# Two more wq tiles through the B stage, six w_mod tiles kept on chip, and zero fills dealt anew

## Chip, cores and metric

The kernel runs on one core of one Trainium2 chip. The metric is device time in microseconds (us), median of several executions. Time before: 603.9 us.

## The reference

One decode token goes through a conditioned transformer layer, forward and backward; all gradients are outputs.

```python
mod = (silu(c) @ w_mod).reshape(6, 1024)            # sa, ca, ga, sb, cb, gb
h = layernorm(x) * (1 + ca) + sa
q = h @ wq                                          # 1024 x 4096, 32 heads
x1 = x + ga * (softmax(q k^T) v @ wo)               # window of 4096 keys, 4 kv heads
h = layernorm(x1) * (1 + cb) + sb
out = x1 + gb * ((sigmoid(h @ w_gate) * (h @ w_up)) @ w_down)
# outputs: out, and the gradients of x, k_cache, v_cache, wq, wo, w_gate, w_up, w_down, c, w_mod
```

The gradients of the two caches have 65536 rows for each head, of which 4096 are not zero. The kernel writes those zeros itself, in 120 transfers of 1 MB, here called **fills**. They depend on nothing, so they are dealt over the program as cover: wherever other transfers are few, fills keep the DMA queue busy.

## The kernel before

Everything lives in one on-chip arena of 192 KB a partition; regions are reused as soon as they are free. Stages in order: q and the scores, the N stage (k^T p v for each head), the B stage, folds and the first modulation products, seven feed-forward rounds, the end (gradients of wo, w_mod, wq, and the two caches' windows). Fills are dealt by constants:

```python
NBP = 6                                    # wq tiles that go through B
Z_N = spread(29, 128)                      # fills beside the 128 steps of N
Z_B = spread(29, 43) + [1, 1, 1, 1, 0]     # beside the 48 chunks of B
Z_FOLD = (3, 2, 2)
Z_FFN = [(1, 1, 1, 1)] * 5 + [(1, 1, 2, 2), (2, 2, 1, 1)]   # four places in each round
Z_END = (2, 1, 1, 0, 0)                    # the first stands before the first wo gradient
```

A chunk of B is eight 512-column matmuls, and a fill can hang on one of them:

```python
def bch(n=1):
    ...
    for a in range(4):
        for k in range(2):
            mm = nc.tensor.matmul(bbank[p][k], lhsT=a4[:, p, 4*u+a, :], rhs=wo_t[u][:, a, k*512:(k+1)*512], ...)
    zero(Z_B[nbq - 1 - len(bq)], recent(mm, 3))
```

Section 5 of w_mod (eight tiles of 256 KB, for gb) is loaded once before N and once again at the end:

```python
wm_sec(5, 0, 8, 160)                       # before N; gb in one product
...
def sec(j):                                # at the end, eight times
    w5 = sec_t[j][:, 3*D:4*D]              # filled by sec_load(j)
    ttr(w5, w5, dmod_b4[:, 3*D:4*D], dcs[:, j:j+1])
    outer_dve(sec_t[j], cs_col[:, j:j+1], dmod_b4)
    nc.gpsimd.dma_start(out=dwm_view[:, j, 2*D:6*D], in_=sec_t[j])
```

Below is the joint between the last feed-forward round and the end. A **side unit** is a small job that is put between other work to fill idle engines: eight transposes on TensorE and one copy on ScalarE (`side(n)` runs n of them).

```python
    else:
        zero(z[2] + z[3])                  # last round
side(len(jobs))                            # left-over transposes, each PE + an ACT copy
for p in range(NBP):
    nc.scalar.copy(out=B_t[p], in_=BT_ps[p])        # parked B tiles out of PSUM
dx1b, m2 = layernorm_bwd_col(dln2, ...)             # sum over partitions on TensorE
bcast(dattn_bf, KD, dattn_b, "AV")
# 64 "do" matmuls that read all wo tiles
zero(Z_END[0]); sec_load(0); ...; sec_load(1)
for u in range(4): dwo(u)                  # overwrite the wo tiles and store them, 1 MB each
```

Of the kernel before, what the change touches and what calls it, by code (L numbers as in the profile page):

```python
# [10 lines left out]
P = 128  # L11
# [8 lines left out]
D = 1024  # L20
# [4 lines left out]
HQ = 32  # L25
# [15 lines left out]
def spread(total, n):  # L41
    return [(i + 1) * total // n - i * total // n for i in range(n)]


NBP = 6
NT = 8
NGA = 9
Z_GA = 3
Z_CB = 3
Z_Q = [0] * 6 + [1, 3]  # L50
Z_KC = [0] * 8
Z_SM = 4
Z_N = spread(29, 128)
Z_B = spread(29, 43) + [1, 1, 1, 1, 0]
Z_FOLD = (3, 2, 2)
Z_FFN = [(1, 1, 1, 1)] * 5 + [(1, 1, 2, 2), (2, 2, 1, 1)]
Z_END = (2, 1, 1, 0, 0)
@with_exitstack
def kernel(
# [266 lines left out]
    wo_t = [ar(o, 8).rearrange("p (a n) -> p a n", a=4) for o in wo_off]  # L326
    B_off = [156, 158, 152, 154, 156, 158]
    junk = vt([P, D], "junk", BF16)
    B_t = [ar(o, 2) for o in B_off[:5]] + [junk]

# [9 lines left out]

    def mod_tiles(ps, tiles, ts_, first):
        for t in ts_:
            for k in range(KD):
                nc.tensor.matmul(ps[:, k:k + 1], lhsT=tiles[t][:, k * P:(k + 1) * P],
                                 rhs=cs_bf[:, t:t + 1], start=(first and t == ts_[0] and k == 0), stop=(t == KD - 1),
                                 skip_group_check=True)
# [136 lines left out]
    for ch in range(8):  # L483
# [9 lines left out]
        zero(Z_KC[ch], mm)  # L493
    g_t = [ar(160 + 2 * t, 2) for t in range(KD)]
    wm_sec(5, 0, 8, 160)
    load_wo(2)
    mx = vt([P, 1], "mx")
    nc.vector.reduce_max(out=mx, in_=mx8, axis=AX.X)
# [108 lines left out]

    def mod_gb():
        ps = new_ps("g_ps")
        mod_tiles(ps, g_t, range(KD), True)  # L610
        cp(gb, ps[:, 0:KD])
        mulv(dffn_bf, go_col, gb)
        load_wo(0)
        load_wo(1)

# [8 lines left out]
    for g in range(G):  # L624
        nbank = bank_pair("n_ps", g)
        for t_ in range(KT):
# [14 lines left out]
            if s == 2:  # L641
                ok_cols(ok4)
            elif s == 4:
                ok_rows()
            elif s == 24:
                mod_gb()
            elif t_ % 2 == 1:
                side()
# [23 lines left out]
    chunks(4, range(8))  # L672
    chunks(5, range(8))
    nbq = len(bq)
    bbank = {}
# [96 lines left out]
    nc.scalar.activation(out=warm, in_=ones_f[:, 0:1], func=ACT.Sigmoid)  # L772
    bch(len(bq) - 16)
    b_sec(4, 0, 16)
# [29 lines left out]
    b_sec(3, 0, 32)  # L804
    park(2, pna, "na")
    park(3, pna, "na")
    v = A3_ps[:, 0:48].rearrange("p (j n) -> p j n", j=KD)
# [18 lines left out]
    bch(5)  # L826
    assert not bq
    b_sec(3, 4, 40)
    zero(Z_CB)
    rot[:] = [(psum, "mm"), (prq, "rq")]  # L830

    def tr_unit(blk):
        def run():
            tp = new_tp("tp_side")
            for i in range(8):
                nc.tensor.transpose(tp[:, i * P:(i + 1) * P], blk[:, i * P:(i + 1) * P], ident_bf[:, :])  # L836
            nc.scalar.copy(out=blk, in_=tp[:, :])  # L837
        return run

    jobs[:] = [tr_unit(v_nat[:, i // 4, (i % 4) * 1024:(i % 4 + 1) * 1024]) for i in range(16)]  # L840
    side(1)
    park(4, ppq, "pq")
    side(3)

# [29 lines left out]

    def fold_tile(t):
        w2 = w2_t[t]
        for k in range(2):
            ps = new_ps("fold_ps")
            for i in range(4):
                nb = 4 * k + i  # L880
                for x, src in enumerate((ga_t[t], cb_t[t], sb_t[t])):
                    nc.tensor.matmul(ps[:, i * P:(i + 1) * P], lhsT=src[:, nb * P:(nb + 1) * P], rhs=ident_bf[:, :],
                                     start=(i == 0 and x == 0), stop=(x == 2), skip_group_check=True)
            fold_ps.append(ps)
        for k in range(2):
            nc.scalar.copy(out=w2[:, k * 512:(k + 1) * 512], in_=fold_ps[k][:, :])
        fold_ps.clear()

    load_wd(0, 0)
    load_wd(0, 1)  # L890
    fold_ps = []
    md_ps = new_acc("md_ps")
    for t in range(4):
        fold_tile(t)
    mod_tiles(md_ps, sb_t, range(4), True)
    load_ug(0, 0, 4)
    load_ug(0, 4, 4)
    zero(Z_FOLD[0])
    side(2)
    mod_tiles(md_ps, sb_t, range(4, 8), False)  # L900
    cp(sb_, md_ps[:, 0:KD])
    h2 = vt([P, KD], "h2")
    mulv(h2, ln2, cb1)
    addv(h2, h2, sb_)
    h2_bf = vt([P, KD], "h2_bf", BF16)
    cp(h2_bf, h2)
    for t in range(4, 8):
        fold_tile(t)
    park(5, prq, "rq")
    rot[:] = [(psum, "mm")]  # L910
    load_ug(1, 0, 4)
    load_ug(1, 4, 4)
    zero(Z_FOLD[1])
    bcast(dffn_bf, KD, b1k, "AV")

# [57 lines left out]
    for h in range(HQ):  # L973
        jobs.append(tr_unit(wo_t[h // 4][:, h % 4, :]))
    for g in range(G):
        jobs.append(tr_unit(N_sb[:, g * 1024:(g + 1) * 1024]))
# [14 lines left out]
    for q in range(NB):  # L991
        z = Z_FFN[q]
        more = q + 1 < NB
        for j in range(KD):
            w = ug_v[:, q % 2, j // 4, j % 4, :, :].rearrange("p k f -> p (k f)")
            ttr(w, w, dug_b, dh2acc[:, q * KD + j:q * KD + j + 1])
            if j in (0, 2, 5) or (j == 6 and q < 4):
                side()
            outer_act(w, h2[:, j:j + 1], dug_b)
            if j == 0:  # L1000
                if q == 0:
                    cp(ffn, ffn_ps)
                else:
                    addv(ffn, ffn, ffn_ps)
            if j == 3:
                store_ug(q, 0, 4)
                zero(z[0])
            if j == 5:
                store_ug(q, 4, 2)
# [31 lines left out]

    B_t = [ar(o, 2) for o in (40, 42, 44, 152, 154, 156)]
    for p in range(NBP):
        nc.scalar.copy(out=B_t[p], in_=BT_ps[p][:, :])
# [52 lines left out]
    def sec(j):  # L1097
        w5 = sec_t[j][:, 3 * D:4 * D]
        ttr(w5, w5, dmod_b4[:, 3 * D:4 * D], dcs[:, j:j + 1])
        outer_dve(sec_t[j], cs_col[:, j:j + 1], dmod_b4)  # L1100
        nc.gpsimd.dma_start(out=dwm_view[:, j, 2 * D:6 * D], in_=sec_t[j])
# [52 lines left out]

    zero(Z_END[0])
    sec_load(0)
    do_ps = new_ps("do_ps")[:, 0:HQ]
    dov = do_ps.rearrange("p (b a h) -> p b a h", b=2, a=4)
    for b in range(2):
        for hh in range(4):  # L1160
            nc.tensor.matmul(dov[:, b, :, hh], lhsT=do_sb[b][:, hh * P:(hh + 1) * P], rhs=ident_f[:, 0::32],
                             start=True, stop=True)
    sec_load(1)
    for u in range(4):
# [20 lines left out]
    dcs234 = matvec_T(lambda jb, nb: w2_t[jb][:, nb * P:(nb + 1) * P], dh2_hl, "dcs234")  # L1185
    for j in range(2, 5):
        sec_load(j)
    dh1b_ps = new_acc("dh1b_ps")
    for j in range(NBP, NT):
        for h in range(HQ):  # L1190
            nc.tensor.matmul(dh1b_ps[:, j:j + 1], lhsT=a4[:, j, h, :], rhs=do_bf[:, h:h + 1],
                             start=(h == 0), stop=(h == HQ - 1))
    for j in range(5, 8):
        sec_load(j)
    dwo(6)
    sec(0)
    cp(dh1[:, NBP:NT], dh1b_ps[:, NBP:NT])
    DO_hd = make_hd(lambda g: do_pv[:, g, :], "DO_hd")
# [23 lines left out]
    addv(dx0, dx0b, dx1)  # L1222
    sec(3)
    for ch in range(8):
        ps = new_ps("dp_ps")
# [90 lines left out]
```

## Time and profile before

| | before |
|---|---|
| time, median | 603.9 us (603.5 to 605.1) |
| profiled span | 602.8 us |
| moved | 248.19 MB, mean 412 GB/s |
| busiest engine | TensorE, 65% of the span |
| first w_up/w_gate product | at 293.5 us |
| first wo gradient stored | at 486.7 us |

The page gives the busy share of the DMA engines in 40 slices; the table of windows gives busy time by stage; the chain and the timeline give single instructions. The prediction below shows these lines.

### The profile page before, as it was taken

How to read it: one execution, taken by the hardware profiler on the slowest of the kernel's cores; microseconds unless marked ns; L12 is line 12 of the kernel's file. 1: busy time of each engine (PE TensorE's matmuls, PEld its weight loads, DVE VectorE, ACT ScalarE, POOL GpSimd, SP SyncE). 2: the span in 40 equal slices, each digit the busy share in tenths (PEclk: the TensorE clock that was granted, in tenths of full speed). 3: DMA queues.
4: the chain of work that ended last, by engine and by line, in shares of the span. 5: the costliest groups of instructions: out<-in, count | busy, mean ns of one | idle time of the engine just before them, and what ended most of it. 6: DMA issues, size and time to landing. Idle time of an engine off the chain costs nothing.

```text
span 602.8 us, 10936 instructions
## 1 busy us (share of the span) xinstructions
PE 389.8 (65%) x4516; PEld 265.6 (44%) x4516; DVE 324.8 (54%) x616; ACT 282.8 (47%) x426; POOL 174.2 (29%) x281
## 2 busy tenths in 40 slices
PE   3997789999999989989433434352533377837200
PEld 3995434334344445548433433342433255736200
DVE  3654498999511010060374675846768279678510
ACT  2489514567202014218273847657476834744100
POOL 0002121212322212213334454455443431132230
PEclk9999699999999989989755555555555586655555
DMA  8999999999999999999999999999999999999996
GB/s 351 421 417 421 406 426 413 413 417 422 421 422 427 423 426 419 407 426 417 406 413 411 412 415 413 413 409 410 414 416 421 422 419 411 423 424 426 424 415 256
DMA packets 47730, 248.19 MB, mean 412 GB/s; under 512 B 5629, under 2 KB 5629, under 8 KB 27264
## 3 DMA queue, kind: packets, MB, share of 16 engines
q0 software_dynamic: 37792, 210.78, 91.0%
q1 hardware_dynamic: 9840, 36.71, 18.0%
q8 instruction: 35, 0.57, 0.4%
q14 instruction: 15, 0.12, 0.1%
q10 hardware_dynamic: 48, 0.01, 0.0%
HBM read 61.87 MB, written 185.60 MB: 411 GB/s over the span
## 4 chain that ended last, share of the span: by engine, by line
DMA 35%; PE 34%; DVE 14%; issue 7%; ACT 5%; POOL 2%; ACTq 0%; POOLq 0%; DVEq 0%; SPq 0%
DMA out_dram<-arena 17%; PE b_ps L687 14%; DMA out_dram<-zeros 8%; DMA arena<-in_B_w_down_dram 7%; PE n_ps L635 6%; DVE arena L210 4%; DVE arena L193 4%; PE t_ps L597 2%; DMA arena<-in_B_w_up_dram 2%; DVE arena L206 2%; DVE junk L210 2%; ACT arena L241 2%; PE tp_wq L453 2%; PE w_ps L394 1%; PE tp_k L434 1%
## 5 line engine op out<-in xcount | busy, mean ns | idle before, releaser
L169 POOL DMA_DIRECT2D out_dram<-zeros x112 | 61.1, 546 | 205.6 <-PE q_ps L471 50.2
L687 PE MATMUL b_ps<-arena 128*128 128x512 bf16 x384 | 89.5, 389 | 0.0
L836 PE MATMUL tp_side<-ident_bf,arena 128*128 128x128 bf16 x416 | 50.1, 297 | 53.7 <-ACT arena L837 44.6
L193 DVE TENSOR_TENSOR arena<-arena 128x2048 bf16<-128x2048 bf16 x64 | 76.6, 1224 | 2.2 <-PE n_ps L635 0.3
L837 ACT COPY arena<-tp_side 128x1024 bf16<-128x1024 bf16 x52 | 52.0, 1010 | 46.0 <-PE tp_side L836 45.8
L210 DVE CUSTOM_DVE_ANT_0 arena<-arena,scr 128x1024 bf16<-128x1024 bf16 x56 | 65.2, 1221 | 9.5 <-ACT scr L970 9.5
L635 PE MATMUL n_ps<-arena 128*128 128x512 bf16 x256 | 65.7, 378 | 6.5 <-DVE arena L193 4.8
L836 PEld LDWEIGHTS <-arena 128*128 128x128 bf16 x416 | 41.2, 137 | 59.2 <-issue 59.1
L241 ACT ACTIVATE arena<-scr,h 128x1024 bf16<-128x1024 bf16 x56 | 61.0, 1146 | 0.0
L687 PEld LDWEIGHTS <-arena 128*128 128x128 bf16 x384 | 37.7, 100 | 46.4 <-issue 7.1
L873 POOL DMA_DIRECT2D out_dram<-arena x42 | 30.7, 733 | 43.9 <-ACT arena L241 36.7
L635 PEld LDWEIGHTS <-arena 128*128 128x128 bf16 x256 | 24.6, 97 | 41.8 <-issue 16.4
L210 DVE CUSTOM_DVE_ANT_0 junk<-arena,b1k 128x1024 bf16<-128x1024 bf16 x28 | 34.3, 1223 | 15.9 <-DMA arena<-in_B_w_down_dram 15.4
L1137 ACT ACTIVATE arena<-ps_kv 128x512 bf16<-128x512 f32 x48 | 26.2, 694 | 29.8 <-PE ps_kv L1133 26.0
L599 ACT CAST arena<-t_ps 128x512 bf16<-128x512 f32 x56 | 30.1, 589 | 12.1 <-PE t_ps L597 12.1
L1133 PE MATMUL ps_kv<-junk,arena 8*128 8x128 bf16 x256 | 27.5, 306 | 10.1 <-DVE arena L206 9.4
L1133 PEld LDWEIGHTS <-arena 8*128 8x128 bf16 x256 | 25.5, 141 | 11.9 <-issue 11.9
L202 DVE CAST arena<-b_ps 128x512 bf16<-128x512 f32 x5 | 3.5, 692 | 47.1 <-PE b_ps L687 47.1
L933 PE MATMUL fg<-h_bf,arena 128*128 128x1 bf16 x448 | 15.6, 166 | 19.0 <-DMA arena<-in_B_w_up_dram 12.4
L455 ACT COPY arena<-tp_wq 128x1024 bf16<-128x1024 bf16 x23 | 21.7, 1044 | 8.0 <-PE tp_wq L453 8.0
L950 PE MATMUL fg<-hh_bf,arena 128*128 128x1 bf16 x224 | 8.0, 166 | 24.1 <-DMA arena<-in_B_w_down_dram 23.4
L933 PEld LDWEIGHTS <-arena 128*128 128x128 bf16 x448 | 14.4, 105 | 20.2 <-DMA arena<-in_B_w_up_dram 13.0
(297 smaller groups left out, 640.0 us busy)
## 6 DMA issues: line engine op xcount, KB each, us to landing
out_dram<-zeros POOLq DMA_DIRECT2D x112, 1024.0 KB, 13.9
out_dram<-arena POOLq DMA_DIRECT2D x32, 1024.0 KB, 18.8
out_dram<-arena POOLq DMA_DIRECT2D x36, 512.0 KB, 10.3
arena<-in_A_wq_dram SPq DMA_DIRECT2D x8, 1024.0 KB, 20.0
out_dram<-zeros POOLq DMA_DIRECT2D x8, 960.0 KB, 13.1
arena<-in_B_w_down_dram SPq DMA_DIRECT2D x14, 512.0 KB, 9.7
out_dram<-arena POOLq DMA_DIRECT2D x28, 256.0 KB, 10.9
arena<-in_A_wo_dram SPq DMA_DIRECT2D x6, 1024.0 KB, 24.8
```

Source lines behind the costliest of these rows:

```text
L169: ins = nc.gpsimd.dma_start(out=region.bitcast(FP32), in_=zeros[:, :])
L193: return nc.vector.tensor_tensor(out=out, in0=a, in1=b, op=op)
L210: return nc.vector.tensor_tensor_reduce(out=out, in0=w, in1=b, scale=1.0, scalar=0.0, op0=ALU.mult, op1=ALU.add, accum_out=acc)
L241: return nc.scalar.activation(out=out, in_=b, func=ACT.Copy, scale=col)
L599: nc.scalar.copy(out=o, in_=ps)
L635: mm = nc.tensor.matmul(nbank[k][:, :], lhsT=k_nat[:, g, t_ * DH:(t_ + 1) * DH], rhs=vp[:, t_ % 2, 4 * k:4 * k + 4, :].rearrange("p h d -> ...
L687: mm = nc.tensor.matmul(bbank[p][k][:, :], lhsT=a4[:, p, h, :], rhs=wo_t[u][:, a, k * 512:(k + 1) * 512], start=(i == 0 and a == 0), stop= ...
L836: nc.tensor.transpose(tp[:, i * P:(i + 1) * P], blk[:, i * P:(i + 1) * P], ident_bf[:, :])
L837: nc.scalar.copy(out=blk, in_=tp[:, :])
L873: nc.gpsimd.dma_start(out=ug_part(view, q, j0, n), in_=ug_tile(q, k, j0, n))
L933: nc.tensor.matmul(gu[:, col + i:col + i + 1], lhsT=ug_v[:, q % 2, j // 4, j % 4, k, f0:f0 + 255:2], rhs=h2_bf[:, j:j + 1], start=(j == 0) ...
L1133: nc.tensor.matmul(ps[:, t4 * DH:(t4 + 1) * DH], lhsT=rows[32 * g:32 * g + HG, t_ * P:(t_ + 1) * P], rhs=hd[32 * g:32 * g + HG, :], start= ...
```

## The change

It means to save the second load of six section-5 tiles. For that it needs a place to keep them through the feed-forward rounds. It gets one by sending wq tiles 6 and 7 through B as well, which frees their 16 KB a partition before the rounds. The gradient part of those two tiles then comes out of B and not out of a second product at the end. The fills are dealt anew for the longer B stage.

```diff
-NBP = 6
+NBP = 8
-Z_CB = 3
+Z_CB = 1
-Z_N = spread(29, 128)
-Z_B = spread(29, 43) + [1, 1, 1, 1, 0]
-Z_FOLD = (3, 2, 2)
-Z_FFN = [(1, 1, 1, 1)] * 5 + [(1, 1, 2, 2), (2, 2, 1, 1)]
-Z_END = (2, 1, 1, 0, 0)
+Z_N = spread(31, 128)
+Z_B = spread(29, 43) + [1, 1, 1, 1, 0] + [1, 1, 0, 1, 1, 0, 1, 1] + [1, 1, 1, 0, 1, 0, 0, 0]
+Z_FOLD = (0, 4, 3)
+Z_FFN = [(1, 1, 0, 1)] * 5 + [(1, 1, 1, 1), (1, 2, 1, 1)]
+Z_END = (1, 1, 1, 0, 0)
...
-    g_t = [ar(160 + 2 * t, 2) for t in range(KD)]
-    wm_sec(5, 0, 8, 160)
+    g_t = [ar(o, 2) for o in (48, 50, 52, 54, 56, 58, 160, 162)]
+    wm_sec(5, 6, 2, 160)
...
+    chunks(6, range(8))
+    chunks(7, range(8))
...
+    fold_run(range(4), 8)            # folds of w2 with B chunks between them
+    wm_sec(5, 0, 4, 48)              # where wq tile 6 stood
...
+    fold_run(range(4, 8), 6)
+    mod_gb((0, 1, 2, 3))
+    wm_sec(5, 4, 2, 56)              # where wq tile 7 stood
+    load_ug(1, 0, 4); load_ug(1, 4, 4); zero(Z_FOLD[1])
+    side(3)
+    mod_gb((4, 5))
+    mulv(dffn_bf, go_col, gb)
...
-        w5 = sec_t[j][:, 3 * D:4 * D]
+        w5 = g_t[j] if j < 6 else sec_t[j][:, 3 * D:4 * D]
-    sec_load(0)          # and 1 to 5, spread over the first wo gradients
...                      # the second dh1 product (64 matmuls) goes, sec_load(6) and (7) stay
```

More of the change, by code (lines that the diff above doesn't have):

```diff
@@ L326 @@
     wo_t = [ar(o, 8).rearrange("p (a n) -> p a n", a=4) for o in wo_off]
-    B_off = [156, 158, 152, 154, 156, 158]
+    B_off = [156, 158, 152, 154, 156, None, 158, 60]
     junk = vt([P, D], "junk", BF16)
-    B_t = [ar(o, 2) for o in B_off[:5]] + [junk]
+    B_t = [junk if o is None else ar(o, 2) for o in B_off]
     def wo_dram(t, u):
@@ L339, in wm_sec, with mod_tiles @@
                             in_=wm_view[:, j:j + n, sct * D:(sct + 1) * D])
-    def mod_tiles(ps, tiles, ts_, first):
+    def mod_tiles(ps, tiles, ts_, first, last=KD - 1):
         for t in ts_:
@@ L344, in mod_tiles @@
                 nc.tensor.matmul(ps[:, k:k + 1], lhsT=tiles[t][:, k * P:(k + 1) * P],
-                                 rhs=cs_bf[:, t:t + 1], start=(first and t == ts_[0] and k == 0), stop=(t == KD - 1),
+                                 rhs=cs_bf[:, t:t + 1], start=(first and t == ts_[0] and k == 0), stop=(t == last),
                                  skip_group_check=True)
@@ L493 @@
         zero(Z_KC[ch], mm)
-    g_t = [ar(160 + 2 * t, 2) for t in range(KD)]
-    wm_sec(5, 0, 8, 160)
+    g_t = [ar(o, 2) for o in (48, 50, 52, 54, 56, 58, 160, 162)]
+    wm_sec(5, 6, 2, 160)
     load_wo(2)
+    load_wo(1)
     mx = vt([P, 1], "mx")
@@ L606, with mod_gb @@
     dffn_bf = vt([P, KD], "dffn_bf", BF16)
-    def mod_gb():
+    def mod_gb(ts_):
         ps = new_ps("g_ps")
-        mod_tiles(ps, g_t, range(KD), True)
-        cp(gb, ps[:, 0:KD])
-        mulv(dffn_bf, go_col, gb)
-        load_wo(0)
-        load_wo(1)
+        mod_tiles(ps, g_t, ts_, True, ts_[-1])
+        if ts_[0] == 6:
+            cp(gb, ps[:, 0:KD])
+        else:
+            addv(gb, gb, ps[:, 0:KD])
     ok4 = ok_sums()
@@ L645 @@
             elif s == 24:
-                mod_gb()
+                mod_gb((6, 7))
+                load_wo(0)
             elif t_ % 2 == 1:
@@ L772 @@
     nc.scalar.activation(out=warm, in_=ones_f[:, 0:1], func=ACT.Sigmoid)
-    bch(len(bq) - 16)
+    bch(len(bq) - 32)
     b_sec(4, 0, 16)
@@ L804 @@
     b_sec(3, 0, 32)
-    park(2, pna, "na")
-    park(3, pna, "na")
     v = A3_ps[:, 0:48].rearrange("p (j n) -> p j n", j=KD)
@@ L826, with tr_unit @@
     bch(5)
-    assert not bq
     b_sec(3, 4, 40)
     zero(Z_CB)
-    rot[:] = [(psum, "mm"), (prq, "rq")]
-    def tr_unit(blk):
+    def tr_unit(blk, dst=None):
         def run():
@@ L836, in run @@
                 nc.tensor.transpose(tp[:, i * P:(i + 1) * P], blk[:, i * P:(i + 1) * P], ident_bf[:, :])
-            nc.scalar.copy(out=blk, in_=tp[:, :])
+            nc.scalar.copy(out=blk if dst is None else dst, in_=tp[:, :])
         return run
-    jobs[:] = [tr_unit(v_nat[:, i // 4, (i % 4) * 1024:(i % 4 + 1) * 1024]) for i in range(16)]
-    side(1)
-    park(4, ppq, "pq")
-    side(3)
     wg_view = B_w_gate.rearrange("(j p) n -> p j n", p=P)
@@ L873, in store_ug, with fold_half, fold_run @@
             nc.gpsimd.dma_start(out=ug_part(view, q, j0, n), in_=ug_tile(q, k, j0, n))
-    def fold_tile(t):
-        w2 = w2_t[t]
-        for k in range(2):
-            ps = new_ps("fold_ps")
-            for i in range(4):
-                nb = 4 * k + i
-                for x, src in enumerate((ga_t[t], cb_t[t], sb_t[t])):
-                    nc.tensor.matmul(ps[:, i * P:(i + 1) * P], lhsT=src[:, nb * P:(nb + 1) * P], rhs=ident_bf[:, :],
-                                     start=(i == 0 and x == 0), stop=(x == 2), skip_group_check=True)
-            fold_ps.append(ps)
-        for k in range(2):
-            nc.scalar.copy(out=w2[:, k * 512:(k + 1) * 512], in_=fold_ps[k][:, :])
-        fold_ps.clear()
-    load_wd(0, 0)
-    load_wd(0, 1)
-    fold_ps = []
+    def fold_half(t, k):
+        ps = new_ps("fold_ps")
+        for i in range(4):
+            nb = 4 * k + i
+            for x, src in enumerate((ga_t[t], cb_t[t], sb_t[t])):
+                nc.tensor.matmul(ps[:, i * P:(i + 1) * P], lhsT=src[:, nb * P:(nb + 1) * P], rhs=ident_bf[:, :],
+                                 start=(i == 0 and x == 0), stop=(x == 2), skip_group_check=True)
+        nc.scalar.copy(out=w2_t[t][:, k * 512:(k + 1) * 512], in_=ps[:, :])
+    def fold_run(tiles, n):
+        units = [(t, k) for t in tiles for k in range(2)]
+        for i, (t, k) in enumerate(units):
+            if (i + 1) * n // 8 > i * n // 8:
+                bch(1)
+            fold_half(t, k)
+    h2 = vt([P, KD], "h2")
     md_ps = new_acc("md_ps")
-    for t in range(4):
-        fold_tile(t)
+    fold_run(range(4), 8)
     mod_tiles(md_ps, sb_t, range(4), True)
@@ L897 @@
     load_ug(0, 4, 4)
-    zero(Z_FOLD[0])
-    side(2)
+    wm_sec(5, 0, 4, 48)
+    park(2, pna, "na")
+    park(3, pna, "na")
+    load_wd(0, 0)
+    bch(2)
     mod_tiles(md_ps, sb_t, range(4, 8), False)
     cp(sb_, md_ps[:, 0:KD])
-    h2 = vt([P, KD], "h2")
     mulv(h2, ln2, cb1)
@@ L906 @@
     cp(h2_bf, h2)
-    for t in range(4, 8):
-        fold_tile(t)
-    park(5, prq, "rq")
-    rot[:] = [(psum, "mm")]
+    fold_run(range(4, 8), 6)
+    mod_gb((0, 1, 2, 3))
+    assert not bq
+    wm_sec(5, 4, 2, 56)
     load_ug(1, 0, 4)
@@ L913 @@
     zero(Z_FOLD[1])
+    park(4, ppq, "pq")
+    park(5, prq, "rq")
+    tr_unit(B_t[6], ar(62, 2))()
+    load_wd(0, 1)
+    jobs[:] = [tr_unit(v_nat[:, i // 4, (i % 4) * 1024:(i % 4 + 1) * 1024]) for i in range(16)]
+    side(3)
+    mod_gb((4, 5))
+    mulv(dffn_bf, go_col, gb)
     bcast(dffn_bf, KD, b1k, "AV")
@@ L974 @@
         jobs.append(tr_unit(wo_t[h // 4][:, h % 4, :]))
+    jobs.append(tr_unit(B_t[7]))
     for g in range(G):
@@ L996 @@
             ttr(w, w, dug_b, dh2acc[:, q * KD + j:q * KD + j + 1])
-            if j in (0, 2, 5) or (j == 6 and q < 4):
+            if j in (0, 2, 5, 6):
                 side()
@@ L1039 @@
     side(len(jobs))
-    B_t = [ar(o, 2) for o in (40, 42, 44, 152, 154, 156)]
-    for p in range(NBP):
+    B_t = [ar(o, 2) for o in (40, 42, 44, 152, 154, 156, 62, 60)]
+    for p in range(6):
         nc.scalar.copy(out=B_t[p], in_=BT_ps[p][:, :])
@@ L1162 @@
                              start=True, stop=True)
-    sec_load(1)
     for u in range(4):
@@ L1185 @@
     dcs234 = matvec_T(lambda jb, nb: w2_t[jb][:, nb * P:(nb + 1) * P], dh2_hl, "dcs234")
-    for j in range(2, 5):
-        sec_load(j)
-    dh1b_ps = new_acc("dh1b_ps")
-    for j in range(NBP, NT):
-        for h in range(HQ):
-            nc.tensor.matmul(dh1b_ps[:, j:j + 1], lhsT=a4[:, j, h, :], rhs=do_bf[:, h:h + 1],
-                             start=(h == 0), stop=(h == HQ - 1))
-    for j in range(5, 8):
-        sec_load(j)
     dwo(6)
     sec(0)
-    cp(dh1[:, NBP:NT], dh1b_ps[:, NBP:NT])
     DO_hd = make_hd(lambda g: do_pv[:, g, :], "DO_hd")
@@ L1223 @@
     sec(3)
+    sec_load(6)
+    sec_load(7)
     for ch in range(8):
```

## The prediction

> **What bounds the kernel now.** I read the slices of the page first, then the table of windows by stage, then the waits, then the timeline of one feed-forward round and of the tail.
>
> The page, whole span in 40 slices of 15.07 us (the first two lines are busy share of the DMA engines and what they moved), and the totals:
>
> ```profile
> DMA  8999999999999999999999999999999999999996
> GB/s 351 421 417 421 406 426 413 413 417 422 421 422 427 423 426 419 407 426 417 406 413 411 412 415 413 413 409 410 414 416 421 422 419 411 423 424 426 424 415 256
> DMA packets 47730, 248.19 MB, mean 412 GB/s; under 512 B 5629, under 2 KB 5629, under 8 KB 27264
> HBM read 61.87 MB, written 185.60 MB: 411 GB/s over the span
> ```
>
> The transfers run at nine tenths or more in 38 of the 40 slices, and at 406 to 427 GB/s whatever the stage. Only the first slice (start-up) and the last (drain) fall short. No engine comes near: the busiest, TensorE, has 65% of the span. 248.19 MB at the 38 full slices' mean of about 417 GB/s take 595 us of a 603 us span. So the kernel is a transfer of 248 MB, with compute arranged beside it.
>
> The same by stage (columns: window, its length, busy us and instructions of PE, PEld, DVE, ACT, POOL; granted clock; DMA share; GB/s):
>
> ```profile
> 60.00:157.00 97.00, 85.39 (x485) 38.44 (x485) 82.91 (x94) 46.84 (x113) 19.95 (x36) 0.95 1.16 416
> 157.00:271.00 114.00, 108.14 (x791) 55.12 (x790) 23.36 (x57) 23.26 (x34) 26.91 (x46) 0.97 1.14 421
> 271.00:293.00 22.00, 18.27 (x324) 16.58 (x323) 0.57 (x4) 15.44 (x23) 8.37 (x14) 1.00 1.16 412
> 345.00:370.00 25.00, 10.63 (x158) 9.14 (x156) 16.38 (x34) 16.27 (x19) 12.03 (x18) 0.50 1.13 413
> 580.00:603.00 23.00, 0.00 (x0) 0.00 (x0) 0.00 (x0) 0.00 (x0) 2.13 (x4) 0.50 0.76 307
> ```
>
> The reader is to see two balances. From 157 to 271 us (the B stage, and the loads and sums beside it) TensorE works 108 of 114 us: this stretch is as long as its matmuls, and the zero fills of the caches are dealt out beside them so that the queue stays full. In one feed-forward round (345 to 370) no engine has more than 16.4 of 25 us: there the transfers set the pace. After 580 nothing computes: the queue drains.
>
> The waits of the whole span say the same from the other side, as the GpSimd queue that issues most transfers waits for earlier transfers:
>
> ```profile
> POOL out_dram L169 <- DMA out_dram<-zeros: 27.0, 16, 2.1
> POOL arena L869 <- DMA out_dram<-zeros: 11.7, 7, 2.2
> ```
>
> A zero fill (L169) reads nothing that a zero fill writes, so I take these waits for room in the queue: the issuer runs up to 2 us ahead of a full queue.
>
> **What the Trainium skill says.** "DMA: Bandwidth & Descriptors", Specifications, names 435 GB/s as the fabric ceiling and about 358 GB/s as the limit of memory for one core. The trace fits the first (427 in its best slice) and not the second (412 over the span), so the measured rate is used. The same page, Anatomy of one DMA, says that DMA engines do not wait on semaphores, that such waits happen on the issuing sequencer; so a late producer shows as an idle issuer, and hurts only if the queue behind it runs empty. Here the issuer does wait for matmuls (38.5 us for b_ps at L169) and the slices stay full. "TensorE: Matmul & The Clock Gate", Part 2, gives 216 ns between 512-column bf16 matmuls; the chain of this kernel shows eight b_ps matmuls in 1.73 us, which is 216 ns. Its Part 1 has the clock halved after idle windows; the trace grants 0.97 in the B stage and 0.50 in the feed-forward rounds, where TensorE is mostly idle, so where matmuls are added matters: these are added where the clock is high.
>
> **The change part by part.**
>
> (a) *Bytes.* Before, section 5 of w_mod (eight 128x1024 bf16 tiles, 262,144 bytes each) is loaded twice: 2 MB before the N stage for gb, and again eight times 256 KB near the end for its gradient. After, tiles 0 to 5 are loaded once, between B and the feed-forward part, and stay; only 6 and 7 are loaded twice. Removed: 6 x 0.262 = 1.57 MB of reads, nothing added. I counted the zero fills from the constants: 119 plus one left for the end before, 120 after; the same 120 regions. 248.19 becomes 246.62 MB. At 417 GB/s: **1.57 / 0.417 = 3.8 us less**, 0.6% of the time.
>
> (b) *Matmuls.* Two more tiles of wq through the B stage: 2 x 8 x 4 x 2 = 128 matmuls of 512 columns in 16 chunks of 1.73 us: **27.7 us more TensorE work**, all before the feed-forward part. Gone: 64 one-column matmuls of the second dh1 sum; the 64 of the gb product in the timeline took 1.59 us, so some 1.6 us, less 16 that are added elsewhere. Two extra transposed tiles (8 transposes, 0.61 us, and a 1.0 us copy each), one in this stretch and one as side work. The gb product is split into pieces of 16, 32 and 16 matmuls; its sum stays 1.6 us, of which 1.2 move behind B. Three side units instead of six run before the feed-forward part (-1.8 us of TensorE). Net for 157 to 293: about +27.5 us.
>
> (c) *What covers those 27.5 us.* The zero fills are dealt anew: N +2, B +10 (33 to 43), the place after B -2, folds -1 before the first feed-forward product and +1 behind it, feed-forward rounds -8 (32 to 24), the end -1, the leftover -1. Between N and the first feed-forward product the queue gets 7 fills (7.34 MB) and 1.57 MB of gb tiles more: 8.9 MB / 0.417 = 21.4 us. That stretch was 136.4 us long (157 to 293.4, the first matmul at L933) with TensorE busy for 126.4; after, 136.4 + 21.4 = 157.8 us of transfers beside some 154 us of matmuls. Compute still fits, with about 4 us to spare instead of 10: the tightest place of the change.
>
> (d) *The rounds get shorter.* A round moves 3.15 MB in, 3.15 MB out and four fills of 1.05 MB: 10.5 MB / 0.413 = 25.4 us, and in the chain the rounds follow each other by 25.2 us (the wait for w_down ends at 352.66 and 377.86). With three fills: 9.44 / 0.413 = 22.9 us. The end loses 1.57 MB of loads and two fills. So B ends late and everything behind it catches up: the shifts are of 20 us and more, the sum is the bytes.
>
> On the path that sets the end lies only (a). The waits removed at the end (the loads before sec) cost nothing today: they are SyncE's, and DVE's longest idle times there are for output tiles to leave.
>
> **Rivals.**
>
> *1. Compute becomes the bound of the rounds.* In the round around 370 us, DVE sits idle 2.84 us until w_down lands:
>
> ```profile
> 371.39 0.16 DVE L193 TENSOR_TENSOR hh_bf<-sg,fg 128x4 bf16<-128x4 f32 x1 [4.47 <-ACT om L939]
> 377.86 1.23 DVE L210 CUSTOM_DVE_ANT_0 junk<-arena,b1k 128x1024 bf16<-128x1024 bf16 x1 [2.84 <-DMA arena<-in_B_w_down_dram]
> ```
>
> Take that and TensorE's 0.90 us wait for w_gate away from 25.2 and the chain through ScalarE's copies and outer products, the gates and DVE's reductions is some 21.5 us. The new round needs 22.9 by bytes. The margin is 1.4 us; rounds 5 and 6 get one more side unit than today (about 1 us on ScalarE) but still have three or more fills. If the chain were 24 us instead, six rounds would lose 6 us and the gain would turn into +3: about 606.
>
> *2. The stretch after B starves the queue.* The last two gb tiles go where tile 7 of wq stood, so their load waits for the last B chunk, and the matmuls for them wait for the load, before dffn, its broadcast and the first round. A load takes some 10 to 14 us to land. Behind it stand two w_up/w_gate loads of 1 MB and four fills, 6.3 MB or 15 us, and 1 MB of w_down: enough cover by my count, so I expect TensorE to stand still there for 5 to 10 us without the queue running dry. If it did run dry, 2 to 5 us would be lost: 602 to 605.
>
> *3. The gain is larger.* Fewer, better placed loads near the end could shorten the drain (307 GB/s in the last 23 us). But the last outputs are the same; I give it 1 us at most: 599.
>
> *4. The removed loads were hidden anyway.* On a queue that is full throughout nothing is hidden: a byte saved is time saved. I reject it; it would leave 603.9.
>
> **Range and chances.** 603.9 - 3.8 = 600.1; a little back for thinner cover (rivals 1 and 2 at part strength) gives 600.4. The range: 598.2 (all of it and a better drain) to 603.6 (nearly all lost to gaps). A gain over 2% would need 12 us, and the whole shortfall of first and last slice plus the bytes is not more than that: 0.01. A loss of over 2% needs 12 us of empty queue: 0.03.
>
> **What would show each step right or wrong.** The page's total should be 246.6 MB with read 60.3 and written 185.6; slices 2 to 39 at nine tenths, 406 to 427 GB/s. 512 b_ps matmuls instead of 384, mean still near 216 ns apart at a clock near 1. The first L933 product at about 315 to 323 us instead of 293; rounds about 23 us apart; no section 5 loads at the end but two. Wrong would be: slices of 7 or 8 around 300 to 325 (rival 2), rounds of over 23.5 us with DMA share falling and DVE's wait for w_down gone (rival 1), a granted clock of 0.5 in the added chunks (27.7 us would become 55 and the queue would run dry), or a rate below 405 GB/s from the new mixture of loads and fills.

## The result

The changed kernel takes **610.06 us** (608.13 to 611.04, six runs) against 603.92 us (603.49 to 605.06, six runs): 1.0% slower, with a ratio of 1.0096 (95% interval 1.0074 to 1.0117). A ratio here is the mean time of one kernel's runs over that of the other's of the same rounds, so not quite the ratio of the two medians. Executions over 1.5% slower than the fastest of the same kernel are left out of the means. The prediction had 600.4 us, and 603.6 at the most.

The page of the changed kernel, the lines that answer to those of before:

```profile
DMA  9999999999999999999999999999999998999996
GB/s 350 420 418 422 415 424 417 425 419 419 423 424 427 423 427 419 417 424 429 400 412 392 423 409 412 410 412 412 412 411 409 377 369 309 407 421 424 424 417 270
DMA packets 46899, 246.64 MB, mean 407 GB/s; under 512 B 5565, under 2 KB 5565, under 8 KB 26432
HBM read 60.30 MB, written 185.60 MB: 406 GB/s over the span
```

The bytes went as predicted, 246.64 MB and 60.30 MB of reads. But there is a trough of 377, 369 and 309 GB/s in slices 32 to 34, from 470 to 515 us, where the kernel before had 411 to 422. It has two parts. The small one is at 475 to 480 us: 294 GB/s, after the issuer had waited 7.45 us for ScalarE. The large one lies behind it; narrow windows of the changed kernel there (window; length; busy us and instructions of PE, PEld, DVE, ACT, POOL; granted clock; DMA share; GB/s):

```profile
490.00:498.00 8.00, 3.05 (x28) 1.53 (x32) 1.71 (x10) 5.49 (x7) 0.00 (x0) 0.50 1.14 425
498.00:502.00 4.00, 4.00 (x99) 2.38 (x92) 2.82 (x7) 1.17 (x2) 0.80 (x1) 0.94 0.06 14
502.00:510.00 8.00, 5.66 (x101) 5.34 (x98) 7.94 (x24) 4.01 (x8) 3.25 (x4) 0.71 0.93 338
510.00:520.00 10.00, 5.50 (x204) 5.25 (x207) 7.60 (x18) 2.12 (x3) 2.60 (x4) 0.50 1.02 372
```

For four microseconds the queue is all but empty, and for another 18 the transfers stay slow. The same place of the kernel before, 15 us earlier in the program's time:

```profile
480.00:490.00 10.00, 9.48 (x141) 5.83 (x141) 7.05 (x23) 3.10 (x6) 3.19 (x5) 0.75 1.14 425
490.00:500.00 10.00, 5.38 (x158) 4.97 (x156) 8.03 (x25) 3.97 (x8) 4.05 (x6) 0.76 1.08 412
```

What GpSimd issued there, from the timeline (start, length, what; in brackets the idle time before it and what ended it). First before:

```profile
478.25 0.53 POOL L169 DMA_DIRECT2D out_dram<-zeros  x1 [1.87 <-DMA out_dram<-zeros]
480.69 1.83 POOL L169 DMA_DIRECT2D out_dram<-zeros  x3 [1.91 <-DMA out_dram<-zeros]
486.71 0.80 POOL L1106 DMA_DIRECT2D out_dram<-arena  x1 [4.19 <-DVE arena L206]
```

then after:

```profile
482.46 1.45 POOL L868 DMA_DIRECT2D out_dram<-arena  x2 [1.72 <-ACT arena L241]
483.91 2.68 POOL L169 DMA_DIRECT2D out_dram<-zeros  x5
501.15 0.80 POOL L1111 DMA_DIRECT2D out_dram<-arena  x1 [14.56 <-DVE arena L206]
```

Before, the issuer waited for earlier transfers (a full queue) and the first wo gradient came 6 us after the last fills. After, five fills went out at once at 483.9 (the issuer had waited for ScalarE, not for the queue), 12.6 us of transfers by 5 x 1.05 MB / 0.417, and then nothing until 501.15. The landing time of the eight wo gradients (issue to landing, min/median/max) tells how much stood in the queue ahead of them, before and after:

```profile
DMA to landing us min/median/max: 14.2/20.4/23.8
```

```profile
DMA to landing us min/median/max: 6.6/9.7/14.3
```

### The account of the shift

Three times from the timelines carry it. The first w_up/w_gate product moves from 293.5 to 321.0 us (+27.5), the first wo gradient from 486.7 to 501.2 (+14.5). So the compute between them took 193.2 us and now takes 180.1: 13.1 less. Of this the rounds gained 17.4 (293.5 to 446.4 before, 321.0 to 456.6 after: from the first product to the long matmul group of the seventh round), and the joint lost about 4. The transfers dealt into that stretch fell by more: eight fills in the rounds and one in front of the first wo gradient less, one more behind the first product, 8 x 1.05 = 8.39 MB, or 20.1 us. 20.1 - 13.1 = **7.0 us without cover**. The profiled run is 3.5 us longer than before and has 3.8 us of bytes less, so 7.3 us went missing.

That the two agree is partly luck: the subtraction leaves out what stood in the queue at either end. The traces allow a direct count. Up to its first wo store the kernel before had moved 202 MB (486.7 us at 415 GB/s), the changed one 206 MB (501.15 us at 411). The 14.4 us more thus moved 4.0 MB, worth 9.6 us at 417 GB/s: some 4.8 us were lost by then and the other 2.5 behind it. These are estimates from rounded rates, good to about 1 us. And the profiled run was the fastest of the six, 608.13 us; on the mean of the runs 5.8 + 3.8 = 9.6 us went missing.

### The profile page after: what moved, and what is told of

Its sections match the earlier page's. It is cut to its first block, busy times and chain, and to the rows that moved or that the text cites.

```text
span 606.3 us, 11103 instructions
## 1 busy us (share of the span) xinstructions
PE 414.7 (68%) x4587; PEld 278.8 (46%) x4612; DVE 326.2 (54%) x619; ACT 285.4 (47%) x430; POOL 176.4 (29%) x283
## 2 busy tenths in 40 slices
DMA packets 46899, 246.64 MB, mean 407 GB/s; under 512 B 5565, under 2 KB 5565, under 8 KB 26432
## 3 DMA queue, kind: packets, MB, share of 16 engines
HBM read 60.30 MB, written 185.60 MB: 406 GB/s over the span
## 4 chain that ended last, share of the span: by engine, by line
PE 43%; DMA 26%; DVE 13%; ACT 10%; issue 5%; POOL 0%; ACTq 0%; POOLq 0%; SPq 0%; DVEq 0%
PE b_ps L691 17%; DMA out_dram<-arena 13%; PE n_ps L636 6%; DMA arena<-in_B_w_down_dram 4%; DMA out_dram<-zeros 4%; ACT arena L241 4%; DVE arena L193 4%; DVE arena L206 3%; DMA arena<-in_w_mod_dram 3%; PE t_ps L598 2%; PE ps_kv L1138 2%; DVE arena L210 2%; PE tp_wq L453 2%; PE w_ps L394 1%; PE fold_ps L875 1%
## 5 line engine op out<-in xcount | busy, mean ns | idle before, releaser
L691 PE MATMUL b_ps<-arena 128*128 128x512 bf16 x494 | 114.4, 381 | 1.2 <-issue 0.4
L836 PE MATMUL tp_side<-ident_bf,arena 128*128 128x128 bf16 x432 | 53.0, 300 | 59.7 <-ACT arena L837 51.6
L837 ACT COPY arena<-tp_side 128x1024 bf16<-128x1024 bf16 x54 | 54.5, 1009 | 39.3 <-PE tp_side L836 38.9
L877 ACT CAST arena<-fold_ps 128x512 bf16<-128x512 f32 x16 | 9.4, 586 | 29.4 <-PE fold_ps L875 29.4
L206 DVE TENSOR_SCALAR arena<-arena,cs_col 128x4096 bf16<-128x4096 bf16 (+1 forms) x16 | 16.0, 1017 | 8.9 <-DMA out_dram<-arena 8.8
```

What stands on the lines that cost most here:

```text
L206: return nc.vector.tensor_scalar(out=out, in0=a, scalar1=s1, scalar2=None, op0=op0)
L691: mm = nc.tensor.matmul(bbank[p][k][:, :], lhsT=a4[:, p, h, :], rhs=wo_t[u][:, a, k * 512:(k + 1) * 512], start=(i == 0 and a == 0), stop= ...
L836: nc.tensor.transpose(tp[:, i * P:(i + 1) * P], blk[:, i * P:(i + 1) * P], ident_bf[:, :])
L837: nc.scalar.copy(out=blk if dst is None else dst, in_=tp[:, :])
```

## The experiments

The changed kernel itself was not timed again beside them; each run was timed against the kernel before on its own chip. I compare runs by their ratios to the kernel before, a hundredth being 6.0 us; the changed kernel stands at 1.0096 (1.0074 to 1.0117). With four runs each, an interval reaches some 1 to 2 us to either side, so smaller differences are called noise unless the runs themselves keep apart. Theory A says that the first wo gradient comes too late and leaves the queue empty; it began with the added matmuls as the cause of the lateness, and that half fell. Its rival, theory B, says that the loss is spread over the dealing of the fills and the late load of the gb tiles, and that the hole is only where it shows.

### 1. Fills of the end moved into the hole

```diff
-Z_END = (1, 1, 1, 0, 0)
+Z_END = (3, 0, 0, 0, 0)
```

> Changed kernel, with the three zero fills of the end stage (1,1,1 before, between and after the first wo gradients) all put before the first of them. Theory A (the added matmuls lengthen the path of compute up to the first wo gradient, about 501 us; the queue, empty from 498 to 502 us there, is refilled only by what is left): the two fills, 5 us of transfers, fall into the gap and leave the later end, so 3 to 5 us faster than the changed kernel's 610: 605 to 607, first wo gradient still stored at 500 to 502 us. Theory B (the loss is spread: thin queue in the feed-forward rounds and before them; the gap is only where it shows): within 1 us of 610.

Measured: 607.14 us (606.71 to 610.74), ratio 1.0070 (1.0036 to 1.0103), or 1.6 us better than the changed kernel by the ratios, which is not clear of noise. The first wo gradient was stored at 502.4. In the profile the hole from 498 to 502 us is closed (422 GB/s), but new ones stand at 510 to 540 us (375, 392 and 348 GB/s), where the two fills now were missing, and at 330 to 340 us (329 GB/s). So closing this hole won little, while the loss reappeared elsewhere; the run alone does not decide between A and B.

### 2. The six tiles loaded again

```diff
-        w5 = g_t[j] if j < 6 else sec_t[j][:, 3 * D:4 * D]
+        w5 = sec_t[j][:, 3 * D:4 * D]
+    sec_load(0) ... sec_load(5)      # at the places of the kernel before
```

> Changed kernel, but the six tiles of section 5 are loaded again at the end, where the kernel before loads them, and used from there: all of the 1.57 MB come back. If bytes on a full queue still set the time (my prediction's step a): 3.8 us slower than the changed kernel, 614. Theory A (the queue is empty or thin from 498 to 520 us, when these loads are issued): they cost nothing or at most 1.5 us: 609 to 611.5.

Measured: 611.69 us (611.43 to 611.9), ratio 1.0128 (1.0113 to 1.0143), so 1.9 us slower than the changed kernel. That is between the two, and the intervals overlap, so how much of the 3.8 us of bytes is hidden stays open. What it does show: with the removed loads put back the kernel is not faster, so their absence is not what opened the hole. Runs 12 and 13 ask about the bytes again on a full queue.

### 3. A quarter of the added matmuls

```diff
-            for a in range(4):
+            heads = range(4) if p < 6 else (0,)
+            for a in heads:
```

> Wrong result on purpose (two columns blocks of one gradient and what follows from them): changed kernel, tiles 6 and 7 of wq do only a quarter of their matmuls in B, so 96 of the 128 added matmuls, 20.7 us of TensorE, go; all transfers and the places of all fills stay. Theory A: the path of compute up to the first wo gradient gets about 20 us shorter as far as the queue lets it, the queue stays full at the joint, and the time falls to what the bytes allow, 600 +- 1.5 us. Theory B (the dealing of the fills and the late load of the gb tiles leave the holes, the matmuls do not): 607 or more.

Measured: 608.87 us (608.13 to 609.38), ratio 1.0080 (1.0065 to 1.0095), only 1.0 us better than the changed kernel and within the noise. Theory A as first put, with the matmuls as its root, failed here; the "607 or more" of theory B came true. The wait view of TensorE in this stretch and the start of the first product say why:

```profile
PE g_ps L344 <- DMA arena<-in_w_mod_dram: 14.5, 2, 13.3
```

```profile
320.31 1.89 PE L938 MATMUL fg<-h_bf,arena 128*128 128x1 bf16 x64
```

With 20.7 us of matmuls gone, the first product still starts at 320.3: TensorE now waits 13.3 us in one go for a gb tile that stands in the queue behind the fills of B. In the changed kernel no such wait is seen: its matmuls end only about when that tile is there. Two limits tie there. That became theory A2: matmuls and transfers together hold the first product, and behind it the compute up to the first wo gradient takes longer than the transfers that are left as cover.

### 4. A shorter path at the joint

No transfer and no fill changes place in the program. The left-over side units and most copies of the parked tiles (B tiles that waited in PSUM) go behind the layernorm sum, the broadcast and the `do` matmuls, and VectorE alone copies the broadcast out. In the changed kernel the broadcast had stood behind those copies:

```profile
494.95 1.01 PE L297 MATMUL bc_ps<-ident_bf,dattn_bf 128*128 128x128 bf16 x8 [6.27 <-ACT arena L1049]
```

```diff
-    side(len(jobs))
-    for p in range(6): nc.scalar.copy(out=B_t[p], in_=BT_ps[p])
+    rot[:] = [(psum, "mm")]
     dx1b, m2 = layernorm_bwd_col(...)
-    bcast(dattn_bf, KD, dattn_b, "AV")
+    bcast(dattn_bf, KD, dattn_b, "VV")
+    for p in range(2): nc.scalar.copy(out=B_t[p], in_=BT_ps[p])
+    rot[:] = [(pgu, "gu"), (px, "x")]
     # do matmuls
+    for p in range(2, 6): nc.scalar.copy(out=B_t[p], in_=BT_ps[p])
+    side(len(jobs))
```

> Changed kernel with a shorter path from the last feed-forward round to the first wo gradient: the four left-over side units and the copies of the parked tiles are moved behind the layernorm sum, the broadcast of dattn and the do matmuls. No transfer and no fill changes place in the program. Theory A: the first wo gradient is stored 8 to 13 us earlier (488 to 493 instead of 501), the queue no longer runs dry, and the time falls by 5 to 9 us: 601 to 605. Theory B: at most 2 us faster, 608 or more.

Measured: 603.86 us (603.44 to 606.2), ratio 1.0006 (0.9987 to 1.0026), 5.4 us better than the changed kernel, clear of noise. What GpSimd issued, and the window where the changed kernel had 14 GB/s:

```profile
484.44 2.68 POOL L169 DMA_DIRECT2D out_dram<-zeros  x5
489.23 0.80 POOL L1114 DMA_DIRECT2D out_dram<-arena  x1 [2.10 <-DVE arena L206]
```

```profile
498.00:502.00 4.00, 4.00 (x29) 4.00 (x27) 0.37 (x5) 0.06 (x1) 0.00 (x0) 0.50 1.04 408
```

The fills go out at the same time as before the edit, the first wo gradient follows 5 us behind them, and the hole is gone. This is the run that shows where most of the loss arose.

### 5. The control: the same shorter path in the kernel before

> Control: the kernel before with the same shorter path from the last feed-forward round to the first wo gradient as in the run that had it on the changed kernel. There the queue was full at that place, so the path was hidden. Theory A (a path of compute costs only where the queue runs dry): first wo gradient about 10 us earlier in the program's order, time within 1 us of the kernel before, 603 to 605. If the path itself sets the time in both kernels: 5 us or more faster, below 599.

Measured: 603.66 us (603.57 to 604.75), ratio 0.9995 (0.998 to 1.001): no change. What GpSimd issued:

```profile
480.69 3.25 POOL L169 DMA_DIRECT2D out_dram<-zeros  x3 [1.76 <-DMA out_dram<-zeros]
483.93 1.52 POOL L1109 DMA_DIRECT2D out_dram<-arena  x2
```

The edit took: VectorE began the first wo gradient at 476.4 us instead of 484.7. But its store stood in the issuer behind the fills, which waited for room, and went out only 2.8 us earlier (483.9 against 486.7), not the 10 that I expected of the program's order. The same path is free where the queue is full and cost 5.4 us where it was empty.

### 6 and 7. Three fills out of B, with a quarter and with all of the matmuls

```diff
-Z_B = spread(29, 43) + ...
-Z_END = (1, 1, 1, 0, 0)
+Z_B = spread(26, 43) + ...
+Z_END = (4, 1, 1, 0, 0)
```

> Wrong result on purpose: a quarter of the matmuls of tiles 6 and 7 in B, and three of the 43 fills of B moved to the place before the first wo gradient. Theory A2 (the first feed-forward product is held at 320 us by two things that end together, the matmuls and the transfers dealt before it; behind it the compute needs 180 us up to the first wo gradient, against 173 us of transfers): with both shortened the first product comes about 7 us earlier, 312 to 314 us, the hole at the joint closes, and the time is 600 to 603. If the dealing had no part: 607 to 609, as with the quarter alone.

> Changed kernel, all matmuls, with the same three fills of B moved to the place before the first wo gradient. Theory A2: the matmuls still hold the first feed-forward product at 318 to 321 us, so the fills that close the hole at the joint open one before the first product: 607 to 611, at most 3 us gained. If the dealing of the fills alone is the cause: the first product 7 us earlier and 601 to 603.

Measured: with a quarter of the matmuls 604.25 us (604.14 to 604.36), ratio 1.0001, a little above the 600 to 603 that I expected; with all of them 605.34 us (605.23 to 606.92), ratio 1.0027. The first product in each, first with all matmuls, then with a quarter:

```profile
317.49 1.89 PE L937 MATMUL fg<-h_bf,arena 128*128 128x1 bf16 x64
```

```profile
313.41 1.89 PE L938 MATMUL fg<-h_bf,arena 128*128 128x1 bf16 x64
```

The tie is borne out: less matmul alone moves the product by 0.7 us, fewer fills alone by 3.5, both by 7.6. (One trace each; in five traces of the same program up to there it starts at 321.0 to 324.4, so the 0.7 means nothing by itself.) But I had given the dealing too little: I expected 607 or more from it alone, and it brought 4.2 us. With fewer fills in B the matmuls cost 1.6 us (1.0027 against 1.0001; no run of the one reaches a run of the other), no more. The three fills close the hole at the joint whether or not the matmuls are there. So two quite different edits, a shorter path (experiment 4) and three fills moved to the joint (7), each close the same hole. What failed is the balance of compute and cover at this joint; the runs do not single out one side of it.

### 8. The compute of one round by itself

```diff
-Z_FFN = [(1, 1, 0, 1)] * 5 + [(1, 1, 1, 1), (1, 2, 1, 1)]
-Z_END = (1, 1, 1, 0, 0)
+Z_FFN = [(1, 0, 0, 1)] * 6 + [(1, 2, 1, 1)]
+Z_END = (1, 1, 1, 0, 7)
```

> Measures the compute of one feed-forward round by itself: changed kernel with two fills a round in the first six rounds, seven moved to the very end. By bytes a round would need 8.39 MB / 0.413 = 20.3 us. My prediction put the compute chain of a round at 21.5 us; the changed kernel shows rounds of 22.6 to 23.6. If the compute of a round is the floor, rounds stay at 22 to 23 us with a DMA share clearly below 1 and no waits for w_down; if 21.5 was right, they fall to 21.5. The time is not of interest (fills that have no cover at the end, some 615 to 625).

Measured, one look of unknown state: 621.58 us, as was to be expected with seven fills without cover. The products start 22.04 us apart on the mean of five (343.20 to 453.42). A round of it, and one of the changed kernel:

```profile
387.00:409.00 22.00, 10.60 (x163) 9.34 (x162) 16.40 (x34) 16.22 (x19) 10.98 (x16) 0.50 1.04 385
```

```profile
387.00:410.00 23.00, 10.10 (x151) 8.66 (x152) 16.48 (x34) 15.56 (x18) 11.42 (x17) 0.50 1.11 412
```

TensorE and VectorE wait for no load in these five rounds. So a round needs 22.0 us of compute, against 21.5 in my prediction. With three fills the bytes need 22.9, and the changed kernel has 23.0 (341.7 to 456.6 over five). The rounds did what I predicted, but they are 1 us from their floor: taking further transfers out of them can win no more than that.

### 9 and 10. Plugging the two smaller holes, two ways

Both have the short path. The first moves two fills from the last round to the places where the issuer then still ran the queue thin (331 and 477 us). The second puts the transposes of v last in the list of side units, runs the left-over ones late, and takes two fills from B.

```diff
# 9                                                 # 10
+Z_FOLD = (0, 5, 3)                                 +Z_B = spread(27, 43) + ...;  Z_FOLD = (0, 6, 3)
+Z_FFN = [(1,1,0,1)]*5 + [(1,1,1,2), (1,1,0,1)]     +Z_FFN = [(1,1,0,1)]*5 + [(1,1,1,2), (1,1,1,1)]
                                                    +    jobs: v transposes last; side(len(jobs)) after dcs234
```

> Changed kernel with the shorter path to the first wo gradient, and two fills moved from the last feed-forward round to the two places where that run's queue still ran thin: one ahead of the first w_down store (a hole of 1.0 us of transfers around 331 us), one ahead of the wait for ScalarE's outer products of the last round (1.2 us around 477 us). If the remaining loss is those two holes (the issuer blocked on a product with too little queued): 1.5 to 2.5 us faster than that run, 601.5 to 602.5. If not: within 0.7 us of it, 603.2 to 604.5.

> The same with more: shorter path at the joint; the sixteen transposes of v all behind the others, so that three leave the path to the first feed-forward product and the left-over units are not needed until late; two fills less in B, two more just before the first product, one moved from the last round to the one before it. If both joints (before the first product and after the last round) cause the loss, the queue should be full throughout and the saved bytes show: first product at 312 to 317 us, 600 to 601.5, that is 3 us better than the kernel before. If the first joint has no part: 601.5 to 602.5, as the plugged run.

Measured: 603.34 us (602.62 to 604.39), ratio 0.9988, and 604.58 us (601.6 to 605.6, so a spread of 4 us over four runs; the profile is of the one of 605.43), ratio 1.0002. Run 9 closed the later of its two holes; the earlier one only moved to 335 us, as its first product came at 324.6; and another opened at 500 to 520 us (367 GB/s). I put that one down to its left-over units, which stand before the `do_ps` matmuls. Run 10, with those units later, has 413 GB/s there, but has a new hole in B: 365 GB/s from 260 to 280 us, 2.5 us of transfers. That the two fills taken from B opened it is not shown: run 7 took three and has 399 and 430 GB/s in these windows. Neither run met its expectation.

### 12 and 13. Full queue, with and without the reload

Run 12 has the dealing of run 9 and the side units of run 10 (no run has the number 11). Run 13 adds the reload of experiment 2.

> Changed kernel with the shorter path at the joint, the dealing of the plugged run, and the order of side units of the run after it (the transposes of v last, the left-over ones late, so that do_ps does not wait behind them and the hole of 2.4 us at 500 to 520 us of the plugged run goes). If holes of an empty queue are all of the loss: 601 to 602, clear of the kernel before. If something else costs time too (the mixture of transfers, the first joint): 603 to 604, no better than the plugged run.

> The same, with the six tiles of section 5 loaded again at the end (1.57 MB more). If bytes set the time wherever the queue is full (my step a): 3 to 4 us slower than the run without the reload. If the loads are hidden even there: within 1 us.

Measured: run 12 takes **602.1 us** (601.9 to 603.27, five runs), ratio 0.9968 (0.9956 to 0.9981); run 13 takes 605.17 us (604.51 to 606.78, 20 runs), ratio 1.0015 (1.0008 to 1.0022). Run 12 is 7.7 us better than the changed kernel and about 2 us better than the kernel before, and is marked correct. (So are runs 3 and 6, which leave out matmuls on purpose; the mark alone proves little.) The page of run 12:

```profile
DMA  8999999999999999999999999999999999999997
GB/s 350 418 418 423 411 426 418 421 417 421 421 424 426 422 427 421 417 427 425 407 415 411 422 385 414 410 412 414 413 397 409 422 417 410 406 407 406 408 407 310
```

The trough is gone (slices 32 to 34 have 422, 417 and 410). And 1.57 MB more cost 2.8 us by the ratios, where 1.57 / 0.417 = 3.8 was predicted, against 1.9 us in the changed kernel. With the queue kept full, these bytes brought most of their worth in time. The 602.1 is within 0.1 us of the 601 to 602 that I expected if holes were all of the loss.

## Why the prediction was wrong

- **(a) Bytes: right.** 246.64 MB against 246.62 predicted, and 60.30 read. Their worth was 2.8 us of the 3.8 where the queue is full (run 13 against 12).
- **(b) Matmuls: right in size, and no cause.** The chunks kept 1.73 us, at a granted clock of 0.98 from 257 to 309 us. Taking three quarters of the added ones away won 1.0 us, within the noise.
- **(c) First joint: nearly right.** The first product was predicted at 315 to 323 us and came at 321.0. I wrote that compute fits "with about 4 us to spare"; there was none to be seen: matmuls and transfers ended about together (experiments 3, 6, 7).
- **(d) The step that failed** is its last sentence: "So B ends late and everything behind it catches up: the shifts are of 20 us and more, the sum is the bytes." The rounds came as predicted, 23.0 us. But I never worked out how much could be caught up by the first wo gradient. It was 13.1 us, of 27.5; the transfers dealt into the same stretch had shrunk by 20.1 us. I had counted fills by stage and bytes in total, and not asked at each joint whether the compute up to there takes longer than the transfers up to there. That subtraction on paper would have shown the danger, though not the exact loss: how much the kernel before had queued in reserve at that moment was not known. (By the count above it was some 3 MB, an estimate: 4.0 MB more had moved in the changed kernel, while only one fill more and one 0.26 MB load less had been dealt.)
- **The joint after the rounds was left out.** The prediction says "On the path that sets the end lies only (a). The waits removed at the end (the loads before sec) cost nothing today". That holds: in the kernel before seven of the eight loads, 1.8 MB, are issued at 489 to 501 us, behind the first wo store, and with six put back the kernel was not faster (experiment 2). What was left out is the compute of the joint. It got about 4 us longer: there was one left-over side unit more (the layernorm sum came 6.0 us after ScalarE's last outer product, before 3.9), and the broadcast waited for ScalarE's copies of the parked tiles. The prediction counts only that three side units leave the first joint (experiment 4 shows what this path is worth).
- **Rival 2** had the right mechanism, a queue without cover at a joint, but named the wrong joint. Against 417 GB/s the windows from 498 to 520 us lack 3.9 + 1.5 + 1.1 = 6.5 us of transfers and 475 to 480 us lacks 1.5; ten-us windows from 290 to 340 us (397, 420, 400, 415 and 394 GB/s) lack 1.4. **Rival 1** did not come true; its chain of 21.5 us measures 22.0. **Rival 4**, that the removed loads were hidden anyway, was rejected on the ground that the queue is full throughout; that ground fell.
- **The idle issuer.** GpSimd's 14.56 us of waiting at L1111 is a wait of the kind that the prediction found harmless where the slices are full. They were full before; for the changed kernel the question had to be asked anew.

**Left open.** The changed kernel's runs fall into two groups, three at 608.1 to 609.2 and three at 610.9 to 611.0 us, and the profiled runs that share its program up to the first product start that product between 321.0 and 324.4 us. I did not find what decides it. Nor is it settled why the rate stays at 338 to 372 GB/s for 18 us behind the empty stretch. Run 12 keeps 1.9 of the 3.8 us; the rest was not traced.

## What to carry to other kernels

Where filler work hides a bound, count it for each stretch between two dependencies and not only in total: for each joint, compare the shortest compute up to it with the transfers that are dealt before it. A path of compute costs nothing until its cover is gone; so when filler is dealt anew for the sake of a byte saving, look for the paths that it had covered, and shorten them (here 5.4 us) or leave them their cover.

## What the Trainium skill lacked or had wrong

- "DMA: Bandwidth & Descriptors", Where 436 GB/s comes from: that the memory side (about 358 GB/s) binds transfers between HBM and SBUF does not hold for this kernel, which runs on one core. It keeps 412 GB/s over 603 us, and 427 in its best slice, three quarters of it writes (185.60 of 247.47 MB). The same page says under its measurements that the 358 is each core's part when both cores of a pair stream; the Specifications row does not repeat that.
- The same page, Anatomy of one DMA: its fit of 2.0 us plus bytes over 436 GB/s gives 4.4 us for a store of 1 MB (an estimate from that page). That is no contradiction, as it is for one transfer by itself: here such stores landed 20.4 us after their issue with a full queue and 9.7 us with a thin one. The page gives no figure for a transfer that stands behind others.
- No page has it: after the queue had run empty, the transfers moved 338 GB/s for 8 us at a DMA share of 0.93, and 372 for 10 us at 1.02, although a 1 MB store was issued every 1.7 us from 501 to 511 us. At the same stage of the kernel before it was 412 to 425 at shares of 1.08 to 1.14, so in this profile a busy share of 1.0 is not the full rate.
